# Attention followed by a soft mixture of experts on one core: the product of the queries' remainder with the keys in bf16

## The chip, the cores and the metric

The kernel runs on one core of one Trainium2 chip. The metric is the device time of one execution in microseconds (us); the time given for a kernel is the median of several runs. Engines are named as in the profile: PE is TensorE, PEld its weight load, DVE is VectorE, ACT is ScalarE, POOL is GpSimd, SP is SyncE.

## The reference

Four batches of 12288 queries attend to keys and values that are the same 768 vectors: 4x4 averages of `kv`, multiplied by `w_sr`. The result goes through a soft mixture of 8 experts with 4 slots each.

```python
kv_pool = kv.reshape(B, H // r, r, W // r, r, C).mean(axis=(2, 4))
k = v = kv_pool.reshape(B, -1, C) @ w_sr          # 4 x 768 x 128
s = scale * (q @ k.transpose(0, 2, 1))            # 4 x 12288 x 768
a = np.exp(s - s.max(-1, keepdims=True))
attn = (a / (a.sum(-1, keepdims=True) + 1e-09)) @ v
...
logits = x @ phi                                  # x = attn as 49152 x 128; 32 slots
slot_input = softmax(logits over rows).T @ x      # then 8 experts: relu(. @ w1) @ w2
out = softmax(logits over slots) @ slot_out
```

## The kernel before

The 49152 queries are worked off in 96 blocks of 512 queries (`BQ`), 24 blocks to a batch. Block `i` has these steps:

- **Scores (`qk`, L544 to L553).** The 768 keys make six tiles `t` of 128. A tile's score is three fp32r products of 128x128 by 128x512 that accumulate in one PSUM bank: high part of the keys by high part of the queries (L551), high part by the queries' remainder (L552), the keys' remainder by the high part (L553). Two tiles share one of three PSUM tiles `s0` to `s2`, so the scores of a block fill all of them. The queries' high part `qhi` is made by ACT (L536), their remainder `qlo` by POOL (L541; by DVE for block 0). Keys are kept per batch as `khi` (ACT, L393 for batch 0, L438 for the others) and `klo` (DVE, L398 and L443), made out of a PSUM bank.
- **Row maximum.** DVE reduces the score tiles (L559, three a block), then L569 and L571; PE multiplies with `sel_r` (L579, called PQ below), and DVE goes on with L584 and L589.
- **Subtraction and exponential.** DVE subtracts (L597, four instructions), which frees the score tiles. ACT takes the exponential twice, as f16 (`phi`, L605) and as fp32 (L609), and POOL makes the remainder `plo` (L614).
- **Product with the values.** PE multiplies `phi` with the high and low part of the values (L631 and L632 in turn; one such pair is called H below) and `plo` with the high part (L639; P below), into two PSUM banks `m0`, `m1`, which PQ and all small products share. One block has 24 H and 24 P; L649 empties the banks.

After every fourth block a group step sums the mixture's statistics (L791 on PE, called G7; POOL, ACT and DVE do the rest). The head of the program pools the keys of batch 0 as they land and makes `khi`, `pooled` (L404) and `klo` of one third after the other, and fills PE with products of ones (L925). The tail (L1222 to L1361) runs the experts and writes the output.

The order on PE, DVE, ACT and POOL is the planner's (class `Plan`): every step has an engine, a cost in us, a priority and dependences, and the planner plays the program through with these costs and emits what it picks. So a changed cost can reorder steps of other kinds. Each engine works strictly in the emitted order.

Of the kernel before, what the change touches and what calls it, by code (L numbers as in the profile page):

```python
# [10 lines left out]
F32R = mybir.dt.float32r  # L11
F16 = mybir.dt.float16
BF16 = mybir.dt.bfloat16
U32 = mybir.dt.uint32
AF = mybir.ActivationFunctionType
# [191 lines left out]
def attention_then_soft_moe(ctx: ExitStack, tc: tile.TileContext, qT, kv0, kvT, w_sr, w_srT, phi, w1, w2, outT):  # L207
# [135 lines left out]
    VBASE = 19.0  # L343
    VSTEP = 1.5
    QKP = 5
    SL = 0.5
    LATE = 6.0
    GAP = 0.55
# [24 lines left out]
    def kv_fold0(h):  # L373
# [2 lines left out]
        nc.vector.tensor_tensor(out=a[:, :n], in0=a[:, :n], in1=a[:, n:], op=ALU.add)  # L376
        kvs[h] = a[:, :n]

    def kv0_mm(h, c, first, end):
        if h == 0 and first:  # L380
            kT[0] = (
                bp.tile([P, NK], F32R, tag="khi", name="khi_0"),
                bp.tile([P, NK], F32R, tag="klo", name="klo_0"),
            )
        if first:
            PK_[0, h] = mt([P, 512], f"pk_0_{h}")
        v = kvs[h] if c is None else kvs[h, c]
        parts = [v[:, o : o + K3] for o in range(0, v.shape[1], K3)]
        for k, x in enumerate(parts):
            nc.tensor.matmul(PK_[0, h][:, :K3], w_sb[:, :C], x, start=(first and k == 0), stop=(end and k == len(parts) - 1))  # L390
# [2 lines left out]
        nc.scalar.activation(kT[0][0][:, h * K3 : (h + 1) * K3], PK_[0, h][:, :K3], AF.Copy, scale=1.0 / R2)  # L393

    def kv0_lo(h):
        hi, lo = kT[0]
        ks = slice(h * K3, (h + 1) * K3)
        nc.vector.scalar_tensor_tensor(  # L398
            out=lo[:, ks], in0=PK_[0, h][:, :K3], scalar=1.0 / R2, in1=hi[:, ks].bitcast(F32),
            op0=ALU.mult, op1=ALU.subtract,  # L400
        )

    def kv0_f(h):
        nc.scalar.activation(pooled[0][:, h * K3 : (h + 1) * K3], PK_[0, h][:, :K3], AF.Copy, scale=1.0 / R2)  # L404

    def kv_acc(b, c):
        if c == 0:
# [16 lines left out]

    def kv_k_mm(b, h):
        if h == 0:
            kT[b] = (
                bp.tile([P, NK], F32R, tag="khi", name=f"khi_{b}"),
                bp.tile([P, NK], F32R, tag="klo", name=f"klo_{b}"),
            )  # L430
        pk = PK_[b, h] = mt([P, 512], f"pk_{b}_{h}")
        k0, k1 = KS[h]
        w = k1 - k0
        nc.tensor.matmul(pk[:, :w], w_sb[:, :C], pooled[b][:, k0:k1], start=True, stop=True)

    def kv_k_hi(b, h):
        k0, k1 = KS[h]
        nc.scalar.activation(kT[b][0][:, k0:k1], PK_[b, h][:, : k1 - k0], AF.Copy, scale=1.0 / R2)  # L438

    def kv_k_lo(b, h):  # L440
        k0, k1 = KS[h]
        hi, lo = kT[b]
        nc.vector.scalar_tensor_tensor(  # L443
            out=lo[:, k0:k1], in0=PK_.pop((b, h))[:, : k1 - k0], scalar=1.0 / R2, in1=hi[:, k0:k1].bitcast(F32),
            op0=ALU.mult, op1=ALU.subtract,
        )
# [84 lines left out]
    def q_hi(i):  # L531
        qsp[i] = (
            qp.tile([P, BQ], F32R, tag="qhi", name=f"qhi_{i}", bufs=2),
            qp.tile([P, BQ], F32R, tag="qlo", name=f"qlo_{i}", bufs=2),
        )
        nc.scalar.activation(qsp[i][0], q_src(i), AF.Copy)  # L536

    def q_lo(i):
        hi, lo = qsp[i]
        eng = nc.gpsimd if i else nc.vector  # L540
        eng.tensor_tensor(out=lo, in0=q_src(i), in1=hi.bitcast(F32), op=ALU.subtract)  # L541


    def qk(i, t):  # L544
        khi, klo = kT[i // BPB]
        hi, lo = qsp[i]
        if t % 2 == 0:
            S[i, t // 2] = ps.tile([P, 2, BQ], F32, tag=f"s{t // 2}", name=f"s_{i}_{t // 2}")
        s = S[i, t // 2][:, t % 2, :]
        ks = slice(t * P, (t + 1) * P)  # L550
        nc.tensor.matmul(s, khi[:, ks], hi, start=True, stop=False)  # L551
        nc.tensor.matmul(s, khi[:, ks], lo, start=False, stop=False)  # L552
        nc.tensor.matmul(s, klo[:, ks], hi, start=False, stop=True)  # L553

    def rowmax1(i, t, n):
        if t == 0:
# [307 lines left out]
    def act(n, aps=0):  # L864
        return n / 1200 + 0.08 + 0.093 * aps
# [65 lines left out]
    def kv_ops(b, base, step, dep0, dep1):  # L931
        kvu = [("kv", b)]
        at_ = {}
        for h in range(2):
            d = dep0[h]
            n = KS[h][1] - KS[h][0]
            p = base + step * h
            at_["k", h] = op("PE", 4 * n / 2400, 0.3, p, d, lambda h=h: kv_k_mm(b, h), acq=[("m", ("pk", b, h))], use=kvu)
            at_["kh", h] = op("ACT", act(n), 0.1, p, [at_["k", h]], lambda h=h: kv_k_hi(b, h), use=[("m", ("pk", b, h))])
            at_["kl", h] = op("DVE", dve(n), 0.08, p, [at_["kh", h]], lambda h=h: kv_k_lo(b, h), use=[("m", ("pk", b, h))])  # L940
            ops["k", b, h] = at_["kl", h]
        vb, vs = base, step
        m = []
        for h in range(2):
            p = vb + vs * (2 + h)
            at_["v", h] = op("PE", 0.85, 0.3, p, dep0[h] + dep1, lambda h=h: kv_v_mm(b, h), use=kvu, acq=[("m", ("pv", b, h))] + ([("v32", b)] if h == 0 else []))
            at_["vo", h] = op("ACT", act(480), 0.1, p, [at_["v", h]], lambda h=h: kv_v_out(b, h), use=[("m", ("pv", b, h)), ("v32", b)])
            for k in range(2):
                m.append(op("ACT", act(3 * (C if k == 0 else NS)) + 0.2, 0.1, p + vs * (1 + 0.4 * k), [at_["vo", h]] + m[-1:], lambda h=h, k=k: kv_a(b, k, h), use=[("v32", b)], raw=0.15))
        kv_s(b, vb, vs, m, dep1)  # L950
# [15 lines left out]
    for h in range(3):  # L966
        mk = ("m", ("pk", 0, h))
        prev = []
        for c in ITEMS[h]:
            first, end = c == ITEMS[h][0], c == ITEMS[h][-1]  # L970
            at, ld = lands[h, c] if c is not None else (0.0, ops["pool", h])
            n = PIECE[h] // 2 if c is None and FOLD[h] else PIECE[h]
            tk = [("t", ("pool", h))] if c is None else []
            prev = [op("PE", 0.43 * n, 0.3 if end else 0.0, -60 + h, prev + [ld], lambda h=h, c=c, first=first, end=end: kv0_mm(h, c, first, end), acq=[mk] if first else [], use=tk + ([] if first else [mk]), at=at)]
        a = op("ACT", act(K3), 0.1, -60, prev, lambda h=h: kv0_hi(h), use=[mk], hot=h == 2)
        ops["k", 0, h] = op("DVE", dve(K3), 0.08, -300, [a], lambda h=h: kv0_lo(h), use=[mk], hot=h == 2)
        a = op("ACT", act(K3), 0.1, -50, [a], lambda h=h: kv0_f(h), use=[mk])
        p = VBASE + VSTEP * h
        mk = ("m", ("pv", 0, h))
        v = [("v32", 0)]  # L980
        m.append(op("ACT", act(K3) + 0.2, 0.1, p + VSTEP, [a] + m[-1:], lambda h=h: kv_a(0, 0, h), raw=0.15))
        a = op("PE", 0.66, 0.3, p, [a], lambda h=h: kv_v_mm(0, h), at=VAT[h], acq=[mk] + (v if h == 0 else []), use=[] if h == 0 else v)
        m.append(op("ACT", act(2 * NS) + 0.2, 0.1, p, [a] + m[-1:], lambda h=h: kv_a(0, 1, h), use=[mk], raw=0.15))
        op("ACT", act(320), 0.1, p, [a], lambda h=h: kv_v_out(0, h), use=[mk] + v)
# [132 lines left out]
    for i in range(NB):  # L1117
# [3 lines left out]
        if o == 0 and g + 1 < NG:  # L1121
            ops["q", g + 1] = op("SP", 0.1, 6.0, T0, [ops["qr", 0]] + ([ops["ql", i - 1]] if i else []), lambda g=g: q_load(g + 1), acq=[("q", g + 1)])
        a = qh = op("ACT", act(BQ), 0.1, T0 - 1.0 * PER, ([qh] if i else []) + ([ops["qr", 0]] if g == 0 and o else [ops["q", g]]), lambda i=i: q_hi(i), acq=[("qs", i)], use=[("q", g)])
        ops["ql", i] = op("POOL" if i else "DVE", 1.28 if i else 0.65, 0.1, T0 - 0.9 * PER if i else -400.0, [a], lambda i=i: q_lo(i), use=[("q", g), ("qs", i)])
        kd = [ops["k", b, x] for x in range(2 if b else 3)]
        for t in range(NT):
            u = t // 2
            ops["qk", i, t] = op(
                "PE", 3 * 0.2315, 0.17, T0 - QKP + 0.65 * t, [ops["ql", i]] + kd[: (1 if t < KSPLIT // P else 2) if b else t // 2 + 1] + ([ops["qk", i, t - 1]] if t else [ops["qk", i - 1, NT - 1]] if i else []),
                lambda i=i, t=t: qk(i, t), acq=[(f"s{u}", i)] if t % 2 == 0 else [], use=[("qs", i)] + ([(f"s{u}", i)] if t % 2 else []),  # L1130
            )
            solo = i == 0 and t >= KSPLIT // P
            if t % 2 or solo:
                n = 1 if solo else 2
                rm = ops["r", i] = op(
                    "DVE", dve(n * BQ) + 0.02, 0.08, T0 - 2.0 + 0.65 * t if i or t > 1 else -185.0, [ops["qk", i, t]] + ([ops["qk", i, t - 1]] if n == 2 else []) + ([rm] if t >= n else []),
                    lambda i=i, t=t, n=n: rowmax1(i, t + 1 - n, n), acq=[("r6", i)] if t == n - 1 else [], use=[(f"s{u}", i)] + ([("r6", i)] if t >= n else []),
                )
# [358 lines left out]
```

## Time and profile before

| | us |
|---|---|
| median of 3 runs | 1076.88 (1074.31 to 1077.33) |
| the profiled execution: own time | 1076.02 |
| its span, first to last instruction | 1074.2 |
| PE busy | 1035.9 (96%) |
| DVE busy | 974.4 (91%) |
| POOL busy | 870.1 (81%) |
| ACT busy | 794.8 (74%) |

Busy time of PE is not PE at its peak: matmuls are pipelined, the recorded end of one lies behind the start of the next, and the pace of a row of matmuls is read from their starts, or from the chain of waits, which gives each the time until the next begins. The granted clock of PE was at its full level, 2.4 GHz, for 0.991 of the span on average.

### The profile page before, as it was taken

How to read it: one execution, taken by the hardware profiler on the slowest of the kernel's cores; microseconds unless marked ns; L12 is line 12 of the kernel's file. 1: busy time of each engine (PE TensorE's matmuls, PEld its weight loads, DVE VectorE, ACT ScalarE, POOL GpSimd, SP SyncE). 2: the span in 40 equal slices, each digit the busy share in tenths (PEclk: the TensorE clock that was granted, in tenths of full speed). 3: DMA queues.
4: the chain of work that ended last, by engine and by line, in shares of the span. 5: the costliest groups of instructions: out<-in, count | busy, mean ns of one | idle time of the engine just before them, and what ended most of it. 6: DMA issues, size and time to landing. Idle time of an engine off the chain costs nothing.

```text
span 1074.2 us, 24818 instructions
## 1 busy us (share of the span) xinstructions
PE 1035.9 (96%) x10232; PEld 887.4 (83%) x10232; DVE 974.4 (91%) x1556; ACT 794.8 (74%) x1044; POOL 870.1 (81%) x505
## 2 busy tenths in 40 slices
PE   8999999999999999999999999999999999998984
PEld 5788888888888888988888888988888898887442
DVE  6989999999999999989999999989999999998674
ACT  3777787788777777788777778788778777775463
POOL 1789998889989988889899988889898999884800
PEclk9999999999999999999999999999999999999897
DMA  9234410120146320120145310120110110113498
GB/s 370 106 86 88 114 55 2 41 97 3 41 92 125 70 56 1 41 99 2 41 108 111 85 40 1 41 99 1 41 41 2 41 40 2 40 40 119 157 417 366
DMA packets 16640, 89.16 MB, mean 83 GB/s; under 512 B 1680, under 2 KB 2960, under 8 KB 10384
## 3 DMA queue, kind: packets, MB, share of 16 engines
q1 hardware_dynamic: 12640, 69.47, 17.5%
q0 software_dynamic: 3312, 17.70, 8.7%
q8 instruction: 81, 1.33, 0.5%
q10 hardware_dynamic: 576, 0.41, 0.1%
q14 instruction: 31, 0.25, 0.1%
HBM read 58.87 MB, written 25.17 MB: 78 GB/s over the span
## 4 chain that ended last, share of the span: by engine, by line
PE 93%; DVE 3%; DMA 2%; ACT 1%; issue 1%; SPq 0%; DVEq 0%; ACTq 0%
PE m L631 15%; PE m L639 15%; PE m L632 15%; PE s L551 13%; PE s L553 12%; PE s L552 12%; PE m L791 2%; PE po L1338 2%; PE m L1310 1%; PE m L579 1%; PE m L1316 1%; DMA outT<-o 1%; DMA kv<-kv 1%; ACT o L1345 1%; DVE r L559 1%
## 5 line engine op out<-in xcount | busy, mean ns | idle before, releaser
L614 POOL TENSOR_TENSOR plo<-t,phi 128x1536 f16<-128x1536 f32 x190 | 598.0, 3157 | 99.8 <-ACT t L609 87.2
L605 ACT ACTIVATE phi<-t 128x1536 f16<-128x1536 f32 x192 | 283.5, 1478 | 150.6 <-DVE t L597 150.6
L559 DVE TRANSPOSE_TENSOR_REDUCE r<-s 128x32 f32<-128x1024 f32 x289 | 354.7, 1234 | 7.9 <-PE s L553 1.8
L631 PE MATMUL m<-vhi,phi 128*128 128x161 f16 x2280 | 353.7, 234 | 8.4 <-DVE m L584 5.9
L632 PE MATMUL m<-vlo,phi 128*128 128x160 f16 x2280 | 352.9, 233 | 0.0
L597 DVE TENSOR_TENSOR t<-s,mb 128x1024 f32<-128x1024 f32 (+1 forms) x384 | 341.9, 950 | 6.0
L609 ACT ACTIVATE t<-t 128x1536 f32<-128x1536 f32 x192 | 283.0, 1476 | 1.2
L631 PEld LDWEIGHTS <-phi 128*128 128x128 f16 x2304 | 224.1, 98 | 21.8 <-issue 21.4
L551 PE MATMUL s<-qhi,khi 128*128 128x512 f32 x576 | 237.9, 413 | 0.7 <-DVE t L597 0.3
L632 PEld LDWEIGHTS <-phi 128*128 128x128 f16 x2304 | 225.1, 98 | 10.6 <-issue 10.2
L553 PE MATMUL s<-qhi,klo 128*128 128x512 f32 x576 | 225.6, 392 | 0.0
L552 PE MATMUL s<-qlo,khi 128*128 128x512 f32 x576 | 224.9, 391 | 0.0
L639 PE MATMUL m<-vhi,plo 128*128 128x161 f16 x2280 | 224.9, 234 | 0.0
L639 PEld LDWEIGHTS <-plo 128*128 128x128 f16 x2304 | 171.3, 98 | 2.7 <-issue 2.7
L541 POOL TENSOR_TENSOR qlo<-q,qhi 128x512 fp32r<-128x512 f32 x95 | 126.9, 1336 | 23.2 <-ACT qhi L536 23.2
L553 PEld LDWEIGHTS s<-qhi,klo 128*128 128x128 f32 x576 | 108.1, 188 | 24.2 <-DVE klo L398 0.4
L551 PEld LDWEIGHTS s<-qhi,khi 128*128 128x128 f32 x576 | 108.3, 188 | 22.0 <-issue 2.3
L552 PEld LDWEIGHTS s<-qlo,khi 128*128 128x128 f32 x576 | 108.6, 189 | 19.6 <-issue 0.7
L649 ACT ACTIVATE xl<-m 128x322 f32<-128x322 f32 x189 | 81.5, 431 | 56.9 <-PE m L639 56.7
L589 DVE STREAM_TRANSPOSE mb<-m 128x512 f32<-128x512 f32 x96 | 68.3, 711 | 3.3
L536 ACT ACTIVATE qhi<-q 128x512 fp32r<-128x512 f32 x96 | 59.5, 620 | 3.2 <-DMA q<-qT 2.8
L584 DVE TENSOR_REDUCE m<-m 128x16 f32<-128x64 f32 x96 | 21.5, 224 | 30.6 <-PE m L579 26.5
(177 smaller groups left out, 846.9 us busy)
## 6 DMA issues: line engine op xcount, KB each, us to landing
q<-qT SPq DMA_DIRECT2D x23, 1024.0 KB, 5.1
outT<-o SPq DMA_DIRECT2D x21, 1024.0 KB, 6.7
kva<-kvT POOLq DMA_DIRECT2D x9, 1536.0 KB, 11.5
kva<-kvT SPq DMA_DIRECT2D x3, 1536.0 KB, 12.9
kv<-kv SPq DMA_DIRECT2D x6, 512.0 KB, 6.2
w<-w SPq DMA_DIRECT2D x2, 1536.0 KB, 6.4
w<-w SPq DMA_DIRECT2D x4, 768.0 KB, 4.2
outT<-o SPq DMA_DIRECT2D x6, 512.0 KB, 3.7
```

The lines of the kernel that those rows point to most:

```text
L541: eng.tensor_tensor(out=lo, in0=q_src(i), in1=hi.bitcast(F32), op=ALU.subtract)
L551: nc.tensor.matmul(s, khi[:, ks], hi, start=True, stop=False)
L552: nc.tensor.matmul(s, khi[:, ks], lo, start=False, stop=False)
L553: nc.tensor.matmul(s, klo[:, ks], hi, start=False, stop=True)
L559: nc.vector.tensor_reduce(out=MX[i][:, t : t + n, :].rearrange("p t b -> p (t b)"), in_=S[i, t // 2][:, u : u + n, :].rearrange("p t (b j) ...
L597: nc.vector.tensor_tensor(out=TT_[i, h][:, o : o + n, :], in0=S[i, t // 2][:, u : u + n, :], in1=MX[i].unsqueeze(1).broadcast_to([P, n, BQ ...
L605: nc.scalar.activation(hi, TT_[i, h], AF.Exp, scale=SCALE)
L609: nc.scalar.activation(t, t, AF.Exp, scale=SCALE)
L614: eng.tensor_tensor(out=lo, in0=TT_.pop((i, h)), in1=PP[i, h][0], op=ALU.subtract)
L631: nc.tensor.matmul(px, p, vhi[:, t, :], start=(t == 0 and (i >= AHD or k % 2 == 0)), stop=False)
L632: nc.tensor.matmul(px[:, 1:], p, vlo[:, t, :], start=False, stop=False)
L639: nc.tensor.matmul(px, PP[i, t // TH][1][:, t % TH, ks], vhi[:, t, :], start=False, stop=(t == NT - 1 and (i >= AHD or k % 2 == 1)))
```

## The change

The remainder `qlo` is written as bf16 and no longer as fp32r. A third copy of the keys, `kb` in bf16, is made by ACT out of the same PSUM bank as `khi` (new step `kv0_b` for batch 0; a second pass in `kv_k_hi` for the others). The product of the remainder with the keys takes `kb`, and stands last of the three in a tile, behind the product with `klo`. The two other products stay in fp32r. Of the planner's costs, a tile of scores is now 0.68 us and no longer 0.6945, a remainder on POOL 1.1 and no longer 1.28, and the ACT step of the keys is twice as long; the scores of batch 0 depend on `kb`. From L551 on a line of the changed kernel has a number 7 higher (L551 is L558, L579 is L586, L631 is L638).

```diff
+    QKC = 0.68
+    QLC = 1.1
...
+    def k_new(b):
+        kT[b] = (
+            bp.tile([P, NK], F32R, tag="khi", name=f"khi_{b}"),
+            bp.tile([P, NK], F32R, tag="klo", name=f"klo_{b}"),
+            bp.tile([P, NK], BF16, tag="kb", name=f"kb_{b}"),
+        )
...
+    def kv0_b(h):
+        nc.scalar.activation(kT[0][2][:, h * K3 : (h + 1) * K3], PK_[0, h][:, :K3], AF.Copy, scale=1.0 / R2)
...
     def kv_k_hi(b, h):
         k0, k1 = KS[h]
-        nc.scalar.activation(kT[b][0][:, k0:k1], PK_[b, h][:, : k1 - k0], AF.Copy, scale=1.0 / R2)
+        for part in kT[b][::2]:
+            nc.scalar.activation(part[:, k0:k1], PK_[b, h][:, : k1 - k0], AF.Copy, scale=1.0 / R2)
...
-            qp.tile([P, BQ], F32R, tag="qlo", name=f"qlo_{i}", bufs=2),
+            qp.tile([P, BQ], BF16, tag="qlo", name=f"qlo_{i}", bufs=2),
...
         nc.tensor.matmul(s, khi[:, ks], hi, start=True, stop=False)
-        nc.tensor.matmul(s, khi[:, ks], lo, start=False, stop=False)
-        nc.tensor.matmul(s, klo[:, ks], hi, start=False, stop=True)
+        nc.tensor.matmul(s, klo[:, ks], hi, start=False, stop=False)
+        nc.tensor.matmul(s, kb[:, ks], lo, start=False, stop=True)
...
-            at_["kh", h] = op("ACT", act(n), 0.1, p, [at_["k", h]], lambda h=h: kv_k_hi(b, h), use=[("m", ("pk", b, h))])
+            at_["kh", h] = op("ACT", 2 * act(n), 0.1, p, [at_["k", h]], lambda h=h: kv_k_hi(b, h), use=[("m", ("pk", b, h))])
...
-        a = op("ACT", act(K3), 0.1, -50, [a], lambda h=h: kv0_f(h), use=[mk])
+        kb_ = ops["kb", h] = op("ACT", act(K3), 0.1, -55, [a], lambda h=h: kv0_b(h), use=[mk])
+        a = op("ACT", act(K3), 0.1, -50, [kb_], lambda h=h: kv0_f(h), use=[mk])
```

On PE, at the first score tiles of block 0, before (`ones` are the filling products):

```order
L456 MATMUL m_116<-ident,pooled_117 128x160 x2
L925 LDWEIGHTS ones
L925 MATMUL wm_143<-ones 128x512
L551 MATMUL s_0_199<-qhi_165,khi_151 128x512
L552 MATMUL s_0_199<-qlo_166,khi_151 128x512
L553 MATMUL s_0_199<-qhi_165,klo_152 128x512
```

and with the change:

```order
L932 LDWEIGHTS ones
L932 MATMUL wm_143<-ones 128x512
L558 MATMUL s_0_200<-qhi_166,khi_151 128x512
L559 MATMUL s_0_200<-qhi_166,klo_152 128x512
L560 LDWEIGHTS kb_153
L560 MATMUL s_0_200<-qlo_167,kb_153 128x512
```

The bf16 product stands third, and its weight load is an instruction of its own; the fp32r products load theirs inside the matmul.

On ACT, where the second third of the keys of batch 0 is made, before:

```order
L393 ACTIVATE khi_151<-m_115 128x256 [waits PE_49]
L404 ACTIVATE pooled_117<-m_115 128x256
L477 ACTIVATE rest_0_1_222,am_187<-pooled_117 128x256 [waits Activation_49]
L393 ACTIVATE khi_151<-m_116 128x256 [waits PE_49]
L404 ACTIVATE pooled_117<-m_116 128x256
```

and with the change:

```order
L399 ACTIVATE khi_151<-m_115 128x256 [waits PE_49]
L413 ACTIVATE kb_153<-m_115 128x256
L410 ACTIVATE pooled_117<-m_115 128x256 [waits DVE_49]
L484 ACTIVATE rest_0_1_227,am_190<-pooled_117 128x256 [waits Activation_49]
L399 ACTIVATE khi_151<-m_116 128x256 [waits PE_49]
L413 ACTIVATE kb_153<-m_116 128x256
L410 ACTIVATE pooled_117<-m_116 128x256 [waits DVE_49]
```

`kb` stands between `khi` and `pooled`, and `pooled` now waits for DVE, which is `klo`: DVE and ACT take turns on the bank.

On PE, behind the scores of block 32, before (`phi`, `plo` and the values `vhi`, `vlo`; `rq` is the operand of PQ):

```order
L632 LDWEIGHTS phi_1_4532
L632 MATMUL m_115<-vlo_3312,phi_1_4532 128x160
L579 MATMUL m_116<-rq_4715,sel_r 128x64
L639 LDWEIGHTS plo_0_4534
L639 MATMUL m_115<-vhi_3311,plo_0_4534 128x161
...
L639 MATMUL m_115<-vhi_3311,plo_1_4606 128x161
L631 LDWEIGHTS phi_0_4506
L631 MATMUL m_116<-vhi_3311,phi_0_4506 128x161
```

and with the change:

```order
L639 LDWEIGHTS phi_1_4540
L639 MATMUL m_115<-vlo_3309,phi_1_4540 128x160
L646 LDWEIGHTS plo_0_4546
L646 MATMUL m_115<-vhi_3308,plo_0_4546 128x161
...
L646 MATMUL m_115<-vhi_3308,plo_1_4611 128x161
L586 MATMUL m_116<-rq_4725,sel_r 128x64
L638 LDWEIGHTS phi_0_4515
L638 MATMUL m_116<-vhi_3308,phi_0_4515 128x161
```

PQ has moved behind the six P of the bank, so that the next H, in the bank of PQ, follows it directly. The same was done in blocks 43, 48, 67 and 72. In blocks 33, 49 and 73 G7, which stood right behind the scores, now stands behind PQ and six P. In blocks 3, 4 and 6 PQ stands ahead of the six P that it stood behind.

## Rows read from the trace of the kernel before

**Rows 1.** The page: busy time by engine, and the chain that ended last, by engine and line.

```profile
PE 1035.9 (96%) x10232; PEld 887.4 (83%) x10232; DVE 974.4 (91%) x1556; ACT 794.8 (74%) x1044; POOL 870.1 (81%) x505
PE 93%; DVE 3%; DMA 2%; ACT 1%; issue 1%; SPq 0%; DVEq 0%; ACTq 0%
```

**Rows 2.** Busy time in one stretch of 100 us in the middle of the span: length, then busy time and instructions of PE, PEld, DVE, ACT and POOL, then granted clock, DMA share, GB/s.

```profile
300.00:400.00 100.00, 99.37 (x1028) 88.18 (x1027) 94.35 (x150) 76.54 (x97) 93.88 (x55) 1.00 0.41 89
```

**Rows 3.** The chain of waits in the middle of the span, in order of time: start, us, engine and line. The scores of block 49, and the end of those of block 50.

```profile
505.76 0.27 PE s L551
506.03 0.24 PE s L552
506.26 0.23 PE s L553
506.50 0.23 PE s L551
...
509.24 0.23 PE s L551
...
520.18 0.23 PE s L553
520.41 0.09 PE m L631
520.49 0.07 PE m L632
```

**Rows 4.** PE in order of time in the head: six filling products of bf16 and 512 columns in a row, and the place where one stands ahead of and behind score tiles (start, recorded length; the pace is the distance of the starts).

```profile
7.77 1.46 PE L925 MATMUL wm<-ones 128*128 128x512 bf16 x6
14.88 0.38 PE L925 MATMUL wm<-ones 128*128 128x512 bf16 x1
14.91 0.58 PE L551 MATMUL s<-qhi,khi 128*128 128x512 f32 x1
15.33 0.39 PE L552 MATMUL s<-qlo,khi 128*128 128x512 f32 x1
16.24 0.39 PE L553 MATMUL s<-qhi,klo 128*128 128x512 f32 x1
16.47 0.39 PE L925 MATMUL wm<-ones 128*128 128x512 bf16 x1
```

**Rows 5.** Groups of instructions: weight loads of the f16 and of the fp32r products.

```profile
L631 PEld LDWEIGHTS <-phi 128*128 128x128 f16 x2304 | 224.1, 98 | 21.8 <-issue 21.4 <-ACT t L609 0.3
L552 PEld LDWEIGHTS s<-qlo,khi 128*128 128x128 f32 x576 | 108.6, 189 | 19.6 <-issue 0.7
```

**Rows 6.** Groups: POOL's remainder of the queries, and a POOL instruction of the same size with a plain fp32 result.

```profile
L541 POOL TENSOR_TENSOR qlo<-q,qhi 128x512 fp32r<-128x512 f32 x95 | 126.9, 1336 | 23.2 <-ACT qhi L536 23.2
L836 POOL TENSOR_TENSOR LL<-LL,RM 128x512 f32<-128x512 f32 (+2 forms) x25 | 24.6, 1018 | 0.0
```

**Rows 7.** Who waited for whom: total us, times, longest.

```profile
PE m L631 <- DVE m L584: 5.9, 19, 0.3
```

**Rows 8.** DVE in order of time, from the scores of block 50 to PQ of block 51.

```profile
520.44 1.25 DVE L559 TRANSPOSE_TENSOR_REDUCE r<-s 128x32 f32<-128x1024 f32 x1
...
523.77 3.55 DVE L597 TENSOR_TENSOR t<-s,mb 128x1024 f32<-128x1024 f32 x4
...
531.87 0.23 DVE L571 SCALAR_TENSOR_TENSOR rq<-m,quad 128x64 fp32r<-128x64 f32 x1
532.55 0.23 DVE L584 TENSOR_REDUCE m<-m 128x16 f32<-128x64 f32 x1
```

**Rows 9.** The chain of waits at PQ of block 31.

```profile
332.29 0.09 PE m L579
...
332.40 0.24 DVE m L584
```

**Rows 10.** DVE at PQ of block 49, behind a G7 on PE.

```profile
513.26 0.23 DVE L584 TENSOR_REDUCE m<-m 128x16 f32<-128x64 f32 x1 [0.69 <-PE m L579]
```

**Rows 11.** The chain of waits at the first scores of block 4.

```profile
57.65 0.05 issue
57.70 0.47 PE s L551
```

**Rows 12.** DVE at PQ of block 3.

```profile
55.25 0.22 DVE L584 TENSOR_REDUCE m<-m 128x16 f32<-128x64 f32 x1 [0.75 <-PE m L579]
```

**Rows 13.** The head: ACT, DVE and PE at the last third of the keys of batch 0.

```profile
22.54 0.38 ACT L393 ACTIVATE khi<-m 128x256 fp32r<-128x256 f32 x1 [3.21 <-PE m L390]
22.82 0.38 ACT L404 ACTIVATE pooled<-m 128x256 f32<-128x256 f32 x1
23.23 0.42 DVE L398 SCALAR_TENSOR_TENSOR klo<-m,khi 128x256 fp32r<-128x256 f32 x1 [0.32 <-ACT pooled L404]
23.71 0.50 PE L553 MATMUL s<-qhi,klo 128*128 128x512 f32 x1
24.95 1.31 DVE L559 TRANSPOSE_TENSOR_REDUCE r<-s 128x16 f32<-128x512 f32 x2 [1.29 <-PE s L553]
```

**Rows 14.** Keys of batch 2: the first part of `khi` on ACT, and DVE at both parts of `klo`.

```profile
426.89 0.59 ACT L438 ACTIVATE khi<-m 128x512 fp32r<-128x512 f32 x1
427.51 0.69 DVE L443 SCALAR_TENSOR_TENSOR klo<-m,khi 128x512 fp32r<-128x512 f32 x1
436.93 0.42 DVE L443 SCALAR_TENSOR_TENSOR klo<-m,khi 128x256 fp32r<-128x256 f32 x1 [0.42 <-ACT khi L438]
```

More of the change, by code (lines that the diff above doesn't have):

```diff
@@ L377, in kv_fold0 @@
         kvs[h] = a[:, :n]
+    def k_new(b):
[4 more added lines that the diff above has]
+        )
     def kv0_mm(h, c, first, end):
         if h == 0 and first:
[L381 to L384, printed above, removed]
+            k_new(0)
         if first:
@@ L395, in kv0_lo @@
     def kv0_lo(h):
-        hi, lo = kT[0]
+        hi, lo, _ = kT[0]
         ks = slice(h * K3, (h + 1) * K3)
@@ L426, in kv_k_mm @@
         if h == 0:
[L427 to L430, printed above, removed]
+            k_new(b)
         pk = PK_[b, h] = mt([P, 512], f"pk_{b}_{h}")
@@ L437, in kv_k_hi @@
         k0, k1 = KS[h]
-        nc.scalar.activation(kT[b][0][:, k0:k1], PK_[b, h][:, : k1 - k0], AF.Copy, scale=1.0 / R2)
+        for part in kT[b][::2]:
+            nc.scalar.activation(part[:, k0:k1], PK_[b, h][:, : k1 - k0], AF.Copy, scale=1.0 / R2)
     def kv_k_lo(b, h):
         k0, k1 = KS[h]
-        hi, lo = kT[b]
+        hi, lo, _ = kT[b]
         nc.vector.scalar_tensor_tensor(
@@ L538, in q_lo @@
     def q_lo(i):
-        hi, lo = qsp[i]
+        hi, lo = qsp[i][:2]
         eng = nc.gpsimd if i else nc.vector
@@ L544, in qk @@
     def qk(i, t):
-        khi, klo = kT[i // BPB]
+        khi, klo, kb = kT[i // BPB]
         hi, lo = qsp[i]
@@ L1123, in attention_then_soft_moe @@
         a = qh = op("ACT", act(BQ), 0.1, T0 - 1.0 * PER, ([qh] if i else []) + ([ops["qr", 0]] if g == 0 and o else [ops["q", g]]), lambda i=i: q_hi(i), acq=[("qs", i)], use=[("q", g)])
-        ops["ql", i] = op("POOL" if i else "DVE", 1.28 if i else 0.65, 0.1, T0 - 0.9 * PER if i else -400.0, [a], lambda i=i: q_lo(i), use=[("q", g), ("qs", i)])
+        ops["ql", i] = op("POOL" if i else "DVE", QLC if i else 0.65, 0.1, T0 - 0.9 * PER if i else -400.0, [a], lambda i=i: q_lo(i), use=[("q", g), ("qs", i)])
         kd = [ops["k", b, x] for x in range(2 if b else 3)]
@@ L1128, in attention_then_soft_moe @@
             ops["qk", i, t] = op(
-                "PE", 3 * 0.2315, 0.17, T0 - QKP + 0.65 * t, [ops["ql", i]] + kd[: (1 if t < KSPLIT // P else 2) if b else t // 2 + 1] + ([ops["qk", i, t - 1]] if t else [ops["qk", i - 1, NT - 1]] if i else []),
+                "PE", QKC, 0.17, T0 - QKP + 0.65 * t, [ops["ql", i]] + ([] if b else [ops["kb", t // 2]]) + kd[: (1 if t < KSPLIT // P else 2) if b else t // 2 + 1] + ([ops["qk", i, t - 1]] if t else [ops["qk", i - 1, NT - 1]] if i else []),
                 lambda i=i, t=t: qk(i, t), acq=[(f"s{u}", i)] if t % 2 == 0 else [], use=[("qs", i)] + ([(f"s{u}", i)] if t % 2 else []),
```

## The prediction

> **What bounds the kernel now.** I read the page first: PE is busy for 96% of the span and holds 93% of the chain that ended last, DVE 3% [rows 1]. In a stretch in the middle PE is busy for 99.4 of 100 us at the full clock, DVE for 94, POOL for 94, ACT for 77 [rows 2]. Busy shares of PE say little, so I went to the chain: at the scores each matmul holds it for 0.23 us, and the next begins at once [rows 3]. So PE's own pace sets the end, and a matmul that gets shorter shortens the kernel, unless DVE takes over. Where it already has: 19 times the first H behind PQ waits for L584 of DVE, 5.9 us in all [rows 7]. DVE is then back to back from the last row maximum of the block before (520.44) to the operand of PQ (531.87) [rows 8]; nothing that PE saves inside such a stretch arrives.
>
> The profiled execution took 1076.02 us (span 1074.2), 0.86 below the median of the three runs. The sum is made against 1076.02.
>
> **The tile's matmuls on PE (96 x 6 tiles).** Before, four tiles start 2.74 us apart (506.50 to 509.24), 0.685 each, so 0.228 a product [rows 3]. With the change two fp32r products are left. The third is bf16 with 512 columns: six such products in the head end 1.46 us after the start of the first, the last one recorded with 0.38, so the five distances are 0.216 each [rows 4]. Does changing the number format twice in a tile cost something? fp32r to bf16: 16.24 to 16.47, 0.23, as from fp32r to fp32r. bf16 to fp32r: from the start of the filling product (14.88) to the second product of the tile behind it (15.33) 0.45, which is 0.216 + 0.23 [rows 4]: hidden to about 0.005. So I take 0.228 + 0.230 + 0.221 = 0.679 for a tile in place of 0.686, a gain of 0.007. At the end of a block the bf16 product meets f16 products: 0.216 in place of 0.23 (520.18 to 520.41), and the first product behind it holds the chain for 0.09 where 0.07 is usual [rows 3]; I take 0.014 + 0.010. A block gains 5 x 0.007 + 0.024 = 0.059 us; 96 blocks gain **5.7 us**.
>
> The bounds: at best the load of the fp32r weights behind bf16 is hidden wholly, 0.012 a tile, 7.9 us in all. At worst it is as where f16 products of 160 columns stand ahead of scores: the first two products hold the chain for 0.27 and 0.24, 0.05 more than two others [rows 3]. I take the row of the filling product, since it has the same 512 columns in front of the load.
>
> Beside this, a rule speaks against the change. Here the f16 load takes 98 ns and is fed by products 70 ns apart (0.07 in the chain), the fp32r load 189 ns behind products 228 ns apart [rows 3, 5]: both lie under other matmuls. The Trainium skill, "TensorE: Matmul & The Clock Gate", Part 3, "The mechanism", says that a weight load overlaps with matmuls in flight only when its row group differs. All loads here use all rows, so by it the added loads of `kb` would stand open; the trace does not agree.
>
> **What is lost of it to DVE.** In the 19 stretches of [rows 7] one block's gain is swallowed, since PE only waits longer: 19 x 0.059 = **1.1 us** back.
>
> **The new order on PE.** In five blocks (32, 43, 48, 67, 72) PQ moves behind the six P, directly ahead of an H in the same bank. That is the arrangement of block 31, where the chain goes PQ, L584, H and PE waits about 0.3 us (5.9 over 19) [rows 7, 9]; a PQ that stands ahead of P has these 0.43 us of work as cover, and now that cover is gone. Since PQ alone behind f16 gets a little shorter, I take 0.2 each: **1.0 us** back; bounds 0 and 1.6. In blocks 33, 49 and 73 G7 (1 us of PE) moves behind PQ. There DVE idled 0.69 us for PQ [rows 10]; it now starts its next stretch up to that much earlier, and the wait of 0.3 at its end, two blocks on, should go: 3 x 0.3 = **0.9 us** gained; bounds 0 and 0.9. In blocks 3 to 7 the first score product holds the chain for 0.47 instead of 0.27, PE having waited for DVE's subtraction [rows 3, 11], while DVE had idled 0.75 for PQ [rows 12]. PQ now comes 0.44 earlier in three of them. I take half of 5 x 0.2: **0.5 us** gained; bounds 0 and 1.
>
> **The head.** klo waits for an ACT instruction that ends at 23.20; it is `pooled` before, and `kb` stands in its place, as long (256 columns, 0.38) [rows 13]. So klo comes at the same time, but now the second product of the tile waits for it and not the third, so one product more lies behind the wait: 23.71 plus 0.22 less the savings, about **0.2 us** later for the row maximum at 24.95, which DVE waits for [rows 13]. `pooled` waits for klo and comes some 0.9 later; the values' matmuls that read it stand behind these scores on PE, so nothing on the path waits. Queued behind it on ACT is the high part of the next block's queries, as much later; its cover is DVE, whose last row maximum, PQ and subtraction of block 0 must pass before the next scores have a free tile. Were that cover gone, the head would lose up to these 0.9.
>
> **Keys of the later batches.** Six more ACT instructions of 0.38 to 0.59 us; ACT is busy for 77% [rows 2], and the keys are needed several blocks later. What can hurt is klo, which waits for `kb` on DVE in strict order, with the row maximum behind it. For the first part klo began at 427.51, right after `khi` (426.89 + 0.59) [rows 14]; now it can wait up to 0.5, three times. For the second part DVE idled 0.42 [rows 14]; there the order now puts a row maximum ahead of klo, so this wait goes in two batches. I take zero, between 1.5 lost and 0.8 gained.
>
> **POOL's remainder** goes from 1336 ns to about the 1018 of an fp32 result of the same size [rows 6], 95 times, so 30 us less of POOL (no row shows a bf16 result of POOL; as slow as fp32r would be no change). No PE wait in the list is for POOL, so this is worth nothing.
>
> **The sum.** -5.7 + 1.1 + 1.0 - 0.9 - 0.5 + 0.2 = -4.8; 1076.02 - 4.8 = 1071.2 for the profiled execution. Runs lie up to 0.86 above it in the median; I give half of that back and predict **1071.6 us**, 0.5% below 1076.88.
>
> **The rivals.**
> 1. *Format changes cost on PE.* If the fp32r load cannot start under a bf16 product, each tile pays the 0.05 of the block's start [rows 3] in place of the 0.012: 576 x (0.05 - 0.012) = 22 us slower, 1098. It decides from 0.012 a tile on. For it: only one place in the trace has bf16 ahead of fp32r at the full clock, and its operands are ones. Against: that place shows 0.005 [rows 4].
> 2. *The added loads stand open*, whatever matmul is in front: 576 x 0.098 = 56 us less the 5.7 or so, 1127. Against it is every f16 product here [rows 3, 5]. (By the skill's rule above it would be this.)
> 3. *DVE takes over, or the change does not do what it says.* DVE has only 6% idle in the middle [rows 2]. If it swallows the gain in all groups of four blocks, or bf16 at real data keeps the 0.228, what is left is the new order and the head: 1075 to 1078, no change. Against: DVE's idle time is waiting for PQ, that is for PE [rows 10, 12].
> 4. *The planner's order goes wrong:* PQ at the end of a bank costs 0.3 in many more blocks, because PE now reaches it earlier than its operand: 20 more such waits, 6 us, would make 1077 to 1082. Against: only five such moves are in the order.
> 5. *More gain*, if both the bound of 0.012 a tile holds and the waits of [rows 7, 11] go: 1066 to 1068.
>
> **How the numbers follow.** Forecast (1068.5 to 1075): 0.62. No change (3): 0.20. Format changes: 0.06. Open loads: 0.01. Order: 0.04. More gain: 0.07. About 0.3%, 3.2 us, is what a measurement of this kernel can tell from no change, so faster means below 1073.6: 0.52 of the forecast's 0.62 and the 0.07 make 0.59. Same: the forecast's other 0.10, the 0.20, and half of the order's 0.04 (up to 1080), 0.32. Slower: 0.06 + 0.01 + 0.02 = 0.09. The range goes from 1067 to 1077.5 and leaves out the format changes, the open loads, most of the order's case and parts of the last two, under 0.2 together.
>
> **What would show it.** In the chain of the changed kernel a tile's three products should hold 0.23, 0.23 and 0.22, and the fp32r product behind bf16 no more than 0.23; a first product of 0.27 in every tile is rival 1. The wait of H for L591 (L584 before) should stand at about 20 times and 6 us; 40 times is rival 4. POOL's remainder should be near 1.05 us. The first row maximum of the last tile should start near 25.15. I am wrong if a tile's pace falls and the span does not: then DVE's rows in the middle will show no idle time at PQ.

## The result and the profile of the changed kernel

The changed kernel takes 1081.56 us in the median of seven runs (1079.9 to 1082.71), the kernel before 1076.86 beside it: a ratio of 1.0051 [1.0038, 1.0064], so 4.7 us slower where 5.3 us faster was predicted. The profiled execution took 1082.59 us (span 1080.8), 6.6 above that of before.

First the page: the engines by busy time, the chain that ended last, and the groups of the score products, of the added weight load, of POOL's remainder and of DVE's reduction behind PQ (busy us, mean ns | idle before, releaser). They answer to [rows 1, 5, 6].

```profile
PE 1040.5 (96%) x10138; PEld 801.6 (74%) x10234; DVE 975.2 (90%) x1556; ACT 796.7 (74%) x1053; POOL 868.9 (80%) x505
...
PE 89%; DVE 4%; ACT 2%; DMA 2%; issue 1%; POOL 1%; ACTq 0%; DVEq 0%; POOLq 0%
...
L558 PE MATMUL s<-qhi,khi 128*128 128x512 f32 x576 | 322.3, 560 | 0.9 <-DVE t L604 0.8
...
L559 PE MATMUL s<-qhi,klo 128*128 128x512 f32 x576 | 227.2, 394 | 0.2 <-DVE klo L404 0.2
...
L560 PE MATMUL s<-qlo,kb 128*128 128x512 bf16 x480 | 187.2, 390 | 0.0
...
L560 PEld LDWEIGHTS <-kb 128*128 128x128 bf16 x576 | 55.3, 96 | 156.0 <-issue 156.0
L548 POOL TENSOR_TENSOR qlo<-q,qhi 128x512 bf16<-128x512 f32 x95 | 125.5, 1322 | 24.3 <-ACT qhi L543 24.3
```

PE is as busy as before and still sets the end. The added loads are 96 ns each, and POOL's bf16 result takes 1322 ns, no less than the fp32r one. 96 of the 576 bf16 products have no record; where one is missing the chain gives its time to the product behind it.

The chain at a block's scores answers to [rows 3] (start, us held, what):

```profile
830.94 0.27 PE s L558
831.21 0.24 PE s L559
831.45 0.46 PE s L558
...
832.38 0.23 PE s L558
832.61 0.23 PE s L559
832.83 0.23 PE s L560
833.06 0.23 PE s L558
833.29 0.24 PE s L559
833.53 0.23 PE s L560
833.76 0.23 PE s L558
833.99 0.23 PE s L559
834.22 0.23 PE s L560
834.46 0.23 PE s L558
```

Three tiles take 2.08 us (832.38 to 834.46), 0.693 each, where 0.679 was predicted and before had 0.685. No single product looks long: ten nanoseconds vanish in the rounding of such a list. So I worked out a tile from all starts between 100 and 900 us: from the klo product of a block's first tile to that of its sixth, median of the 52 blocks whose scores run without a break. Before, this is 3.431 us, 0.686 a tile; in the changed kernel 3.469, 0.694.

PE's waits, of the changed kernel and then of before (who waits for whom: us, times, longest):

```profile
PE m L638 <- DVE m L591: 6.5, 21, 0.3
PE m L638 <- ACT xl L656: 3.4, 8, 0.5
```

```profile
PE m L631 <- ACT xl L649: 2.2, 5, 0.5
```

The wait for DVE is nearly as before [rows 7]; the wait for ACT's `xl`, which empties a PSUM bank, comes eight times instead of five.

### The profile page after: what moved, and what is told of

Read it like the earlier page. It is cut to its first block, busy times and chain, and to the rows that moved or that the text cites. A ratio compares the mean times of both kernels' runs of the same rounds, so it can differ in the third digit from the quotient of the medians.

```text
span 1080.8 us, 24765 instructions
## 1 busy us (share of the span) xinstructions
PE 1040.5 (96%) x10138; PEld 801.6 (74%) x10234; DVE 975.2 (90%) x1556; ACT 796.7 (74%) x1053; POOL 868.9 (80%) x505
## 4 chain that ended last, share of the span: by engine, by line
PE 89%; DVE 4%; ACT 2%; DMA 2%; issue 1%; POOL 1%; ACTq 0%; DVEq 0%; POOLq 0%
PE m L638 15%; PE m L646 15%; PE s L558 14%; PE m L639 14%; PE s L559 12%; PE s L560 10%; PE m L798 2%; PE po L1346 2%; DMA outT<-o 1%; DVE t L604 1%; PE m L586 1%; PE m L1318 1%; DMA wT_sb<-w_srT 1%; PE m L1324 1%; PE m L396 1%
## 5 line engine op out<-in xcount | busy, mean ns | idle before, releaser
L638 PE MATMUL m<-vhi,phi 128*128 128x161 f16 x2280 | 353.4, 234 | 10.2 <-DVE m L591 6.5
L558 PE MATMUL s<-qhi,khi 128*128 128x512 f32 x576 | 322.3, 560 | 0.9 <-DVE t L604 0.8
L638 PEld LDWEIGHTS <-phi 128*128 128x128 f16 x2304 | 225.1, 98 | 4.1 <-issue 4.0
L559 PE MATMUL s<-qhi,klo 128*128 128x512 f32 x576 | 227.2, 394 | 0.2 <-DVE klo L404 0.2
L560 PE MATMUL s<-qlo,kb 128*128 128x512 bf16 x480 | 187.2, 390 | 0.0
L560 PEld LDWEIGHTS <-kb 128*128 128x128 bf16 x576 | 55.3, 96 | 156.0 <-issue 156.0
L548 POOL TENSOR_TENSOR qlo<-q,qhi 128x512 bf16<-128x512 f32 x95 | 125.5, 1322 | 24.3 <-ACT qhi L543 24.3
L559 PEld LDWEIGHTS s<-qhi,klo 128*128 128x128 f32 x576 | 109.6, 190 | 12.9 <-issue 0.7
L558 PEld LDWEIGHTS s<-qhi,khi 128*128 128x128 f32 x576 | 114.3, 198 | 3.5 <-PE m L798 1.0
```

The source lines that it names most:

```text
L559: nc.tensor.matmul(s, klo[:, ks], hi, start=False, stop=False)
L560: nc.tensor.matmul(s, kb[:, ks], lo, start=False, stop=True)
L638: nc.tensor.matmul(px, p, vhi[:, t, :], start=(t == 0 and (i >= AHD or k % 2 == 0)), stop=False)
```

## The experiments

Runs are given as a ratio to the kernel before, run beside them (1076.06, 1075.12 and 1074.86 us in the three groups of runs, so times of different groups are compared by their ratios). The part behind the last operand of PQ took 102 to 105 us in all profiles but one (107), with no pattern that the edits explain, so profiles are compared by **body**: the end of that instruction (L571 before) in the last block, less that of before (970.14 us). In every trace the granted clock is 1.00 from 30 us to that point, and 0.90 to 0.97 in the 50 us behind it. The changed kernel has +5.91. A body is that of one execution; how far it varies between executions was not measured.

### Products or order?

The changed kernel with the planner's two costs of before; PE's order is then that of before but for blocks 17 and 19 (and one more filling product in the head):

```diff
-    QKC = 0.68
-    QLC = 1.1
+    QKC = 3 * 0.2315
+    QLC = 1.28
```

> The changed products with the planner's costs of before (0.6945 for a tile, 1.28 for the remainder): the order of PE is that of before but for two blocks. Theory F (each change between fp32r and bf16 holds up PE by 10 to 12 ns): the tile stays at 0.695 us and most of the loss stays, 1079.5 to 1081.5. Theory O (the planner's new order loses it, and the products cost nothing): the loss goes, 1074 to 1077. If both share it, about 1079.

Measured: 1079.2 us, 1.0035 [1.0023, 1.0047]; body +3.31, a tile 0.694.

The kernel before with the new costs alone:

```diff
-                "PE", 3 * 0.2315, 0.17, T0 - QKP + 0.65 * t, ...
+                "PE", 0.68, 0.17, T0 - QKP + 0.65 * t, ...
```

(and 1.28 to 1.1 for the remainder)

> The kernel before, all three products in fp32r, with only the two costs changed (0.68 and 1.1): the new order without the new products. Theory F: as before, 1076 to 1077.5. Theory O: 1080 to 1082. If both share it, about 1079.

Measured: 1080.19 us, 1.004 [1.0026, 1.0054]; body +3.34, a tile 0.686. Its order is not wholly that of the changed kernel: PQ stands elsewhere in blocks 24, 42, 43, 66 and 67. The next run has that order exactly. Which of the two costs moves the steps was not tried.

The changed kernel in its own order, with the products back in fp32r:

```diff
-            qp.tile([P, BQ], BF16, tag="qlo", name=f"qlo_{i}", bufs=2),
+            qp.tile([P, BQ], F32R, tag="qlo", name=f"qlo_{i}", bufs=2),
...
-        nc.tensor.matmul(s, kb[:, ks], lo, start=False, stop=True)
+        nc.tensor.matmul(s, khi[:, ks], lo, start=False, stop=True)
```

> The changed kernel, its order untouched, but the remainder is written as fp32r and the third product takes the high part of the keys in fp32r, last of the three; the bf16 copy of the keys is still made by ACT and read by nobody. No format changes inside a block. Theory F: a tile is back at 0.686 us, 1076 to 1078. Theory O: the loss stays, 1080.5 to 1082. If both share it, 1079.

Measured: 1078.5 us, 1.0031 [1.0019, 1.0043]; body +2.48, a tile 0.687. PE, DVE, ACT and POOL run the steps in the order of the changed kernel.

Neither theory alone holds: both causes are there. The products with the old order cost 3.31, the order with the old products 2.48; 5.79 together, and the changed kernel has 5.91. That they add up so closely may be luck, since each number is of one execution.

How the order's loss arises is seen by following the same point through the blocks (us later than before at the end of L571 of a block):

| block | 0 | 10 | 19 | 22 | 32 | 34 | 48 | 50 | 66 | 68 | 74 | 95 |
|---|---|---|---|---|---|---|---|---|---|---|---|---|
| old products, new order | 0.15 | -0.38 | -0.40 | -0.08 | -0.11 | 0.41 | 0.73 | 1.24 | 1.63 | 1.90 | 2.44 | 2.48 |
| new products, old order | 0.16 | 0.48 | 0.90 | 1.10 | 1.36 | 1.44 | 1.80 | 1.86 | 2.49 | 2.55 | 2.79 | 3.31 |
| changed kernel | 0.47 | 0.29 | 0.59 | 1.08 | 1.37 | 2.01 | 2.65 | 3.23 | 4.20 | 4.47 | 5.29 | 5.91 |

The products' loss grows by 0.03 a block. The order's comes in steps: it gains in blocks 3 to 8, then loses 0.3 at blocks 20 and 21 and 0.5 at each of 32 to 34, 48 to 50 and (with the blocks ahead of them) 72 to 74, where PQ moved behind the six P and G7 behind PQ, and 0.2 to 0.3 at 43 and 67, where PQ alone moved. Another 0.4 comes in small steps between blocks 50 and 66 and was not followed up. The chain of the kernel with the new costs alone, two blocks behind a moved G7:

```profile
533.98 0.38 PE m L639 x5
534.36 0.02 issue
534.38 0.45 ACT xl L649
534.83 0.04 issue
534.87 0.23 PE m L631
```

and that of the changed kernel where PQ itself was moved, at block 48:

```profile
505.60 0.09 PE m L586
505.68 0.02 issue
505.71 0.23 DVE m L591
505.94 0.04 issue
505.98 0.23 PE m L638
```

The first is the place of the wait for L584 which the prediction let vanish (532.55 before, the end of the stretch of [rows 8]): it is gone, and a longer wait for ACT stands there. The second is the wait of about 0.3 that was predicted. So one wait of 0.3 for DVE became one of 0.3 for DVE, at another block, and one of 0.4 for ACT.

### What in the products?

The changed kernel with the bf16 product first in even tiles and last in odd ones:

```diff
+        prods = [(khi, hi), (klo, hi)]
+        prods = prods + [(kb, lo)] if t % 2 else [(kb, lo)] + prods
+        for k, (key, qry) in enumerate(prods):
+            nc.tensor.matmul(s, key[:, ks], qry, start=k == 0, stop=k == 2)
```

> The changed kernel with the bf16 product first in the even tiles and last in the odd ones, so that a block has six changes of format in place of twelve (with the one from f16 at its start and the one to f16 at its end); the order of everything else is that of the changed kernel. Theory F: a tile falls from 0.695 to about 0.684, 6.3 us less of PE over 576 tiles, of which 4 to 6 arrive: 1075.5 to 1077.5. Theory O: as the changed kernel, 1081 to 1082.

Measured: 1073.46 us, 0.9977 [0.9967, 0.9986], 2 us below what was expected; body -2.51, 8.4 less than the changed kernel, whose order it has.

The same with the old costs:

> Both repairs: the bf16 product first in the even tiles and last in the odd ones, and the planner's costs of before (0.6945 and 1.28), so the order of before but for two blocks. Theory that the two causes are separate and both arrive: below the kernel with the old costs (1079.2) by six changes of format a block, 96 x 6 x 0.011 = 6.3 us, and below the one with alternating products (1073.5) by some 2 to 3 of order: 1070 to 1072.5. Rival, that DVE takes over and the faster tile only leaves PE waiting: no better than the alternating one, 1073 to 1075.

Measured: 1072.05 us, 0.997 [0.996, 0.9981]; body -4.37. By the body the order is again worth 1.9; the ratios, 0.9977 and 0.997, have intervals that overlap and leave the size open. Against the kernel with the old costs the faster products arrive nearly wholly: 7.7 us of the body, where the time from a block's last P to the third product behind its scores falls from 4.405 us to 4.319 (medians of the plain blocks, whose scores run without a break), 8.3 in 96 blocks.

With the new costs for the first six blocks alone:

```diff
-                "PE", QKC, 0.17, ...
+                "PE", QKC if i < 6 else 3 * 0.2315, 0.17, ...
```

> As the kernel with both repairs, but the planner takes the new costs (0.68 and 1.1) for the first six blocks and those of before from there on: only the order of blocks 1 to 9 changes. In the two runs with the new order these blocks gained 0.9 us. If that gain stands by itself: 0.9 below the kernel with both repairs, 1069 to 1071.5. If it is only lent and given back at the next wait: the same as that kernel.

Measured: 1071.66 us, 0.9969 [0.9958, 0.998]; body -4.75. Of the early gain about 0.4 stays by the profile; by the medians it is no difference.

The old costs, and the bf16 product in the middle of each tile:

```diff
+        nc.tensor.matmul(s, khi[:, ks], hi, start=True, stop=False)
+        nc.tensor.matmul(s, kb[:, ks], lo, start=False, stop=False)
+        nc.tensor.matmul(s, klo[:, ks], hi, start=False, stop=True)
```

> The costs of before, and the bf16 product in the middle of the three of each tile: 14 changes of format a block (with those from and to the f16 products) in place of the 12 of the kernel with the old costs (1079.2). Theory F, a price of 10 to 12 ns for each change: 96 x 2 x 0.011 = 2.1 us more, of which at least half arrives, 1080 to 1082. Rival, that the price belongs to a tile's beginning (a fp32r load behind the last product of the tile before) and not to the change: the same or less, 1076 to 1079.5.

Measured: 1078.1 us, 1.0033 [1.0021, 1.0045], the same as with the bf16 product last; body +3.82, 0.5 more. A tile is 0.694 as there. The expectation of 1080 or more missed. The two added changes are those from and to f16 at a block's edge. From the last P to the third product behind the scores a plain block does take 4.424 us in place of 4.405, but of the 1.8 us which that makes in 96 blocks the body shows 0.5; whether the two changes cost 11 ns each stays open.

The old costs, and the bf16 product first in every tile:

```diff
+        nc.tensor.matmul(s, kb[:, ks], lo, start=True, stop=False)
+        nc.tensor.matmul(s, khi[:, ks], hi, start=False, stop=False)
+        nc.tensor.matmul(s, klo[:, ks], hi, start=False, stop=True)
```

> The costs of before; the bf16 product stands first in every tile, so a tile still changes format twice, but a block's f16 products meet a bf16 product of 512 columns and the fp32r load stands behind that. In the kernel with both repairs a block took 13 ns for each of the six changes less, or all of it lay at the block's start. Theory F (11 ns for a change wherever it stands): a tile stays at 0.695 us, as the kernel with the old costs, 1078 to 1080. Rival S (the start of a block, where the first two products held the chain for 0.05 more): 96 x 0.045 = 4.3 us less, 1074 to 1075.5.

Measured: 1072.16 us, 0.9973 [0.9963, 0.9983], below even rival S; body -3.67, 7.0 less than with the bf16 product last, although a tile is 0.693 and changes format as often. Its chain at a block's start:

```profile
832.25 0.43 PE m L646 x6
832.68 0.22 PE s L558
832.90 0.24 PE s L559
833.13 0.23 PE s L560
```

The first two products hold 0.22 and 0.24, where fp32r ones behind f16 hold 0.27 and 0.24. From the last P to the third product behind the scores it is 4.370 us in place of 4.405. Where small products break the scores of a block in two, there are two such starts, and that block's period shrinks from 9.75 to 9.56, more than two starts at 0.035 explain. In the steady groups of four blocks it is 0.07 a block (16 blocks: 158.14 to 157.01), 6.8 of the 7.0.

Both bf16 products of a pair of tiles together, first in the first and third pair, last in the second, with the old costs:

```diff
+        u = t - t % 2
+        both = [(kb, lo, u), (kb, lo, u + 1)]
...
+            last = u // 2 % 2 == 1
+            if last and t % 2:
+                own = own + both
+            elif not last and t % 2 == 0:
+                own = both + own
```

> The costs of before; the two bf16 products of a pair of tiles stand together, first in the first and third pair of a block, last in the second, so a block has three changes inside and the one to f16 at its end in place of the six of the kernel with both repairs (1072.05). At 11 ns each, less up to 2 more for the end: 96 x 0.02 to 0.033 = 2 to 3 us less, 1069 to 1070.5. Rival (what was gained came from the block's start, which is as there): 1071.5 to 1073.

Measured: 1070.15 us, 0.9952 [0.994, 0.9965]; body -4.96 although its profiled execution is 1.5 us later than the run with both repairs as early as block 0, having waited longer for a DMA of the weights (1.0 in before):

```profile
PE m L927 <- DMA wT_sb<-w_srT: 2.2, 1, 2.2
```

The row orders give the price of a change. A product takes 0.2287 us in fp32r (before, 3.431 over 15) and 0.2157 in bf16 (all parts in bf16, below: 3.236 over 15). From the klo product of the first tile to that of the sixth:

| kernel | products fp32r + bf16 | at those paces | measured | changes | one change |
|---|---|---|---|---|---|
| bf16 last (changed) | 10 + 5 | 3.366 | 3.469 | 10 | 10 ns |
| bf16 in the middle | 10 + 5 | 3.366 | 3.469 | 10 | 10 ns |
| bf16 first | 10 + 5 | 3.366 | 3.467 | 10 | 10 ns |
| first and last in turn | 10 + 4 | 3.150 | 3.197 | 4 | 12 ns |
| in pairs | 10 + 4 | 3.150 | 3.180 | 2 | 15 ns |

The recorded starts show where most of it lies. In the changed kernel a bf16 product starts 0.236 us behind the klo product ahead of it, 7 ns more than the pace, and the next klo product 0.458 later, 14 more than 0.2157 + 0.2287. Where two bf16 products stand together (first and last in turn), the second is 11 ns late and the way back to fp32r costs 2; where four do (in pairs), the second is 11 late, the next two are on pace, and the way back costs 6. So the product behind the first bf16 one is late in either format. Where it is an fp32r product, the record of its weight load is longer too; in the changed kernel (L558 stands behind the bf16 product, L559 does not):

```profile
L559 PEld LDWEIGHTS s<-qhi,klo 128*128 128x128 f32 x576 | 109.6, 190 | 12.9 <-issue 0.7
L558 PEld LDWEIGHTS s<-qhi,khi 128*128 128x128 f32 x576 | 114.3, 198 | 3.5 <-PE m L798 1.0
```

### Without fp32r

The old costs, with `khi`, `klo`, `qhi` and `qlo` all in bf16. This leaves out precision: the high parts are rounded to bf16 and the remainders are what is left of that, rounded again.

```diff
-            bp.tile([P, NK], F32R, tag="khi", name=f"khi_{b}"),
+            bp.tile([P, 2 * NK], BF16, tag="khi", name=f"khi_{b}")[:, :NK],
```

> The costs of before and all parts of queries and keys in bf16, so no fp32r in the scores (this leaves out precision: each of the four parts is rounded to bf16, and the remainders are those of the rounded parts). No change of format at all between the score products, and a product is 0.216 by the row of the filling products: a tile of 0.650 in place of 0.695, 26 us less of PE. If all of it arrived, 1053. DVE has only some 9 to 10% idle, a part of it at the program's ends: if it takes over in the middle, 1060 to 1068. If only the count of changes mattered and not the pace, about 1072.

Measured: 1058.0 us, 0.9841 [0.9829, 0.9854]; body -18.06, a tile 0.647. That lies between the 1053 of full arrival and the 1060 from which DVE was expected to take over.

The kernel before with the same four parts in bf16, so without the third copy of the keys:

> The kernel before with all four parts of queries and keys in bf16 (this leaves out precision, as the run before with all parts in bf16) and no third copy of the keys: the third product takes the high part again. The order is that of before everywhere. As that run, 1058, less what ACT's extra copies cost: if they cost nothing, 1057 to 1059; if the head's 0.16 to 0.25 and the keys of later batches were theirs, 1056.5 to 1058.

Measured: 1057.28 us, 0.9833 [0.982, 0.9847]; body -19.14, the fastest of all. ACT's copies of the keys cost at most the 1.1 of the body. Of this 0.35 is there in block 0, and 0.22 of that goes with klo's product, which stands third here and stood second there (from the start of the last `khi` to the end of PQ's operand 4.24 us here, 4.46 there). Its chain in a block:

```profile
830.02 0.22 PE s L551
830.23 0.22 PE s L552
830.45 0.22 PE s L553
830.66 0.22 PE s L551
830.88 0.21 PE s L552
831.10 0.22 PE s L553
831.31 0.22 PE s L551
```

The same with the planner's cost of a tile at the pace that the tile now has:

```diff
-                "PE", 3 * 0.2315, 0.17, ...
+                "PE", 0.65, 0.17, ...
```

> The same, with the planner's cost of a tile at 0.65, which is now its measured pace: most blocks get another order. If a true cost lets the planner place the steps where they are due: 1054 to 1057. If it places PQ and the group steps closer to their operands, as with the two changed costs on the kernel before (3 to 4 us lost): 1059 to 1063.

Measured: 1067.06 us, 0.9928 [0.9916, 0.994], so some 10 us are lost again by an order made with the true cost; 1059 to 1063 was too little. Its waits show where:

```profile
PE m L631 <- DVE m L584: 8.5, 26, 0.6
PE m L631 <- ACT xl L649: 7.6, 20, 0.5
```

With the order of before the same products have 5.9 and 0.9 of these two, 9.3 us less in all; the two bodies differ by as much.

## Why the prediction was wrong, by its own steps

**PE's pace sets the end: right.** With all parts in bf16 a block loses 0.293 us between P and H (4.387 to 4.094), 28.1 us in 96 blocks, and 19.1 of it arrive. Most of the rest goes where the prediction said: in the steady groups one block in four keeps its period of 9.77 us in all kernels with an order near that of before, since DVE is idle for only 0.28 us of it; a quarter of 28.1 is 7.0.

**The tile's matmuls: the step that failed.** It read from the filling products in the head that bf16 to fp32r is hidden to about 0.005 and that fp32r to bf16 costs nothing, and took 0.679 for a tile. Measured were 0.694: two changes of 10 ns each take 0.021, the cheaper product gives back 0.013. So -5.7 became +3.3 by the run with the old order: at the pace of the steady groups (16 blocks: 157.75 to 158.15) 2.4 of it, and some 0.2 in the head. The end of a block did what the prediction said: five tiles lose 0.038, and from P to the third product behind the scores it is only 0.018 (4.387 to 4.405), so the end gives back 0.020 where 0.024 was taken. The place in the head that was read stands alone, and its pair gives 0.45 in the changed kernel too, while pairs of real scores take 0.457; why it is cheaper there was not tried. Rival 1 had the mechanism; it was to decide from 0.012 a tile on, and 0.021 was measured. Its price of 0.05 was too high: that row is a start behind f16 products of 160 columns, another place. The best case of 7.9 us should be 8.1 by its own terms, which changes nothing. The 1.1 that was to be lost of the gain to DVE had no gain to be taken from.

**The added loads (rival 2): rejected.** They take 96 ns each and a tile grew by 8 in all. The Trainium skill, "TensorE: Matmul & The Clock Gate", Part 3, "The mechanism", says that a load overlaps with matmuls in flight only when its row group differs (a sentence of the same section also lets loads into the background weight buffer run ahead); by the row group alone all 96 ns would stand open, and the trace does not agree.

**The new order: one term right, one of the wrong sign.** PQ behind P was set at 0.2 each and measured 0.2 to 0.3 at blocks 43 and 67, where it stands alone. G7 behind PQ was to gain 0.3 in three groups; with PQ's own move it lost 0.5 in each. The wait for L584 went as predicted, but what is late next is ACT's `xl`, which the step did not ask for; and G7's other move, with that of small products at blocks 20 and 21, was not in the list of moved steps (0.3). That list also left out PQ at 45 and 69 and small products at 48 and 72; no loss shows at the first two, and none at the others beyond that of blocks 32 to 34. The early blocks' 0.5 is there (-0.53 from block 0 to block 10 in the new order with the old products) but kept to the end only in part. In sum the order was set at -0.4 and measured +2.5. Rival 4 looked for 20 more waits at PQ; there are 2 more, and three for `xl`.

**The small terms.** The head: klo's place costs 0.23, against 0.2. From the start of the last `khi` to the end of PQ's operand it is 4.64 us in the changed kernel and with the old costs, where klo is second of the three, and 4.40 to 4.42 where it is third (before, and with bf16 in the middle or first). The last tile's first row maximum began at 25.42 and not 25.15, since the first scores also began 0.43 later. The keys of later batches: zero was taken, and the loss of the new products with the old order shows no step there larger than 0.25. POOL's remainder stayed at 1322 ns, not 1018, and since no wait is for POOL this changed nothing at run time, as said. The 1018 was misread: it is the mean of three sizes [rows 6]. By size, fp32 results of 128x512 took 1052 to 1307 ns in before (L836, L757), so no gain from a narrower result was shown there. But the 1.1 that the planner was given for this step was too low.

**The test that was named** for rival 1, a first product of 0.27 in every tile, could not have shown it: a change of 10 ns is one in the last digit of the chain. The sum of several tiles shows it.

## What to carry to other kernels

A cheaper format for one of several products in a row is paid for at the changes of format; count the changes and lay equal formats side by side across the borders of tiles, and try which product should meet the foreign stretch. Here it was the bf16 one, whose load is half as long; that the load is the reason was not shown. Here the same three products range from 1079 to 1070 us by their order alone.

A changed number in a planner is a change of its own: time it alone. The new costs of this change were in fact the less true ones (0.68 and 1.1, where 0.694 and 1.322 were measured and 0.6945 and 1.28 had stood), and their order lost 2.5 us. But a true cost can give a worse order too: 0.65 in the last run, which lost some 10.

When a difference of 1% of an instruction matters, take the distance over many of them from the trace, and a price from many places, not from the one that happens to show it.

## What the runs showed of the hardware

- Among products of 512 columns a change between fp32r and bf16 costs PE 10 to 15 ns at the full clock (10, 4 and 2 changes in five tiles: 0.103, 0.047 and 0.030 us). The product behind the first bf16 one is 11 to 14 ns late; the way back from two or four bf16 products costs 2 to 6. What changes to and from f16 at a block's edge cost by themselves stays open.
- Where scores start behind f16 products of 160 columns, a bf16 product of 512 columns put first saves time against one put last: 35 ns in the median of the plain blocks, and 0.19 us of the period of the block whose scores are broken. The chain shows 0.05 of it at the first product (0.27 to 0.22); the end of the scores changes with it, so the start alone was not separated.
- Products of 512 columns follow each other in 0.2157 us in bf16 and in 0.2287 in fp32r, although the records of single ones say 379 and 391 to 413 ns.
- POOL wrote the remainder as bf16 no faster than as fp32r (1322 and 1336 ns for 128x512).
